# The words of w_out in the buffers of the probabilities and of the state product, with a new order of issue

## The chip, the core and the metric

One core of a Trainium2 chip runs the whole kernel in one launch. The metric is the device time of one execution in microseconds (us), as the median of several runs. TensorE is written PE (its weight loads PEld), VectorE DVE, ScalarE ACT, GpSimd POOL, and SyncE SP; SP issues every DMA here.

## What is computed

The kernel fuses a two-way attention between a sequence and a small state with a gated projection over the joined result.

```python
B, H, S, Ns, D = 8, 8, 512, 32, 64
scores  = scale * x @ state.T                 # 512 x 32 for each batch and head
xread   = softmax(scores) @ state
scores2 = scale * state @ x.T
sread   = softmax(scores2) @ x
y = concat([xread, sread], axis=2)            # to (batch, 576, 512)
gate_pre = sum(conv_w[k] * shifted(y, k) for k in range(5))
out = (sigmoid(gate_pre) * (y @ w_val)) @ w_out
```

The three weights w_val, conv_w and w_out arrive as 64-bit floats and are seen by the kernel as 64-bit words.

## The kernel before

A batch is one of eight. Its four x tiles are transposed on PE (`x_T`, tile xT), the scores of the 32 state rows are multiplied out (`long_scores` for batches 0 to 2, `scores` for the others, tile sc), and the softmax along the state rows follows on DVE, POOL and ACT: `scores_T` (tile sl), `max_n` (mx), `sub_n`, `exp_n` (ex), `sum_n` (sm, rc), `scale_n`, and `probs`, which transposes the probabilities back into sl (tile a0 for batch 0). The other softmax runs beside it (`max_s` with nb, `exp_s` with e, `exp_T`, `state_read` with srp). `state_val` (sgv, split into swh and swl) multiplies the state by w_val beforehand, so that `values` needs only the probabilities, split into a high part ah and a low part al. `read` (for batch 0 `read_conv` on z5) gives xr, the five taps of the gate run over it (`gate_first`, `gate_tap`, `gate_last`, `gate_add`, `gate`), `gated` makes the product g, which is split into gh and gl, and `project` multiplies by w_out, split into woh and wol. The last 32 rows of each batch, from sread, are done together at the end (`tail_values`, `tail_project`).

The weights come in as words. `load_words` brings 128 rows of a weight (512 KB) into an SBUF buffer, and five steps turn them into 32-bit floats: `words_scale` on ACT, `words_clamp` on DVE or POOL, and `words_low`, `words_join`, `words_sign` on DVE. A buffer of words is free when `words_sign` has read it. Tiles are made from pools of few buffers, and the table `alias` says which pool a short-lived tile takes its buffer from: "al" and "swl" (two buffers each, 4 KB a partition) hold the low parts of the probabilities and of the state product, "ah" and "swh" (two each, the same size) the high parts, and also a0 and sw0 of batch 0.

Each piece of work is a step with a number. `ORDER` lists the 938 step numbers in the order in which they are issued, with the engine for the steps that can run on several (a is ACT, v is DVE, g is POOL). Each engine runs its instructions in that order, and so does SP with its DMAs; an instruction that waits for a buffer or an operand holds up all that stands behind it on its engine. `warm_up` is a step of four small matmuls that nothing reads; 33 of them stand in the order.

```python
    with tc.manual_schedule(engines=None):
        for step in ORDER:
            engine = ENGINES.get(step[-1])
            fn, args = steps[int(step.rstrip("avg"))]
            fn(*([engine] if engine else []), *args)
```

Of the kernel before, what the change touches and what calls it, by code (L numbers as in the profile page):

```python
# [9 lines left out]
F32 = mybir.dt.float32  # L10
F32R = mybir.dt.float32r
I32 = mybir.dt.int32
# [16 lines left out]
LONG = (0, 1, 2)  # L29
ENGINES = dict(a="ACT", v="DVE", g="POOL")  # L30
ORDER = """
0 50 1 107 10 18 53 11a 65 41 42a 12 5 13g 14 43 23 7 35 44v 15 24a 45 36a 25 37 46 2 6 47 26v 29 915 916 917 918 919
920 921 922 923 924 925 926 927 928 929 930 931 932 933 934 48 114 38v 106 19 104 64a 105 27 39 30a 55a 115a 20a 89
935 112 28 4 113a 52a 31 16 108 185 54a 188 21 110 32v 109a 111a 33 936 120 51a 17 186 116 40 90a 34 189 91 195 49a
22a 122 62 56 191 123 92g 133 187 60v 193 286 118 77 119 287 121 59 285 190a 117 131 58a 288 57a 130 124 139 192a 196a
194a 93 134a 63a 125g 61a 141a 197 198 78a 71 66v 201 132a 184 291 199 94 293 79 103 8 126 292a 135 83 294a 127 68 385
295 296a 202 289 290a 200 388 128g 67a 101a 203 937 297 205 136 142g 129 80v 301 214 145 303 386 204 140a 143 302 299
387 146a 215a 84a 298 206g 486 213 151 207 216 208 304 86v 144 81 209v 85 69 70a 152a 168 137 150 217a 148 72a 82 222
153 147 154 487 155a 87 218 225a 73 284 156 74g 149a 219 210 138a 300 484 169 316 97a 75 88 227 76 211a 317a 228 160
170a 157 230 158a 226 223a 212g 485 95a 224 229a 159v 98g 164 231 165 314 250a 249 171g 235 256 220 583 315a 232 221a  # L40
389 391 390a 395 251 237 233g 166a 392a 252 396a 161 167g 393 394a 318 253 234 313 421 319 422a 397 238 96g 236a 264
257 402 384 423 254g 162a 99a 268 403 398 399 255 260 163g 401 239 400 269 258a 270a 305 100g 424a 102g 242 240v 322
306g 325a 243a 307 413 323a 414a 259g 425 181 326 241 172 244 494 245 182a 320 173a 246 308 309g 324 404 321a 415 261
492 483 493a 247g 495a 488 175 262a 310 263g 327 586 176v 311a 342 312v 343a 178 248 416a 328 405g 335 344 368 265
271g 585 345 346 266a 179a 406 347g 489a 330 356 348 350a 490 337 364 331 174 332 365 267g 329a 349 360 407 338 333g
275 272 682 491a 351 334 276a 339 352 357 520 183 408g 353 409 685 336a 273a 358a 340g 354g 523a 359g 410a 341 274 426
521v 524 281 582 366a 412 177 361 427 428a 584 411g 278 367g 429 522 362a 355 430 434 436 282a 683 496 431 369 363g
437 417 780 497 459 432g 279a 370a 448 435a 498 418 499 500 371g 449a 503 450 455 280 438 451 504g 587 433 456 439g
452 441 378 591 505 440 457a 506 283 507g 453g 501 460 372 588a 373a 684 443 502 508 375 379v 592a 442a 277 525 454
461g 376a 444 445 512 467 526 528 529 589 458g 446g 513a 468 514 593 533 463 509a 515a 447 530 784 462g 781 511 180  # L50
535 527a 381 547 548a 536 590a 419 549 594a 595 537 382a 420a 550 377 464 619 469g 531g 551 510g 465g 532 599 782 534a
692 540 600 470g 596 622a 686 687a 566 601 693a 597 552g 688 620a 598 602 603g 562 553 621 613 690 623 541a 689a 567
554 691a 542 516 466g 604 694 783 517 543 605 699 700 606g 374 544 545g 696 614a 695 607 568a 480 555 481a 697 546
569g 471 482 472a 473 624 608a 791 785 698 538v 610 380 563 639 641 642 643 556a 557g 474 786a 625 9 558 518 539 475a
789 632 701 640a 633v 627 609g 519a 564a 611 634 628 612a 790a 644g 645 681 477 626a 661 635 559 646 636 653 702g 703
478a 560a 648 787 629 565g 712 637g 479 792a 788a 561g 662 649 718 713a 793 881a 719a 615 704 663a 650 797 795 630g
638 616 794 879a 647a 885a 664g 886v 631 573 710 705g 654 798 570 721a 720 651g 800 617 574a 801g 706 711a 722 796
571a 799 809 655a 707a 709 657 618a 723 731 732a 808 714 715 658 733 725a 724 652 579 659a 476 580a 581 726 734 708g
727 716 656g 665 660g 735 810a 811 736g 883a 717a 764 802 745 812a 728 729g 747 666 576 748 667a 730 577a 813 738 803
740 749 817 752 383 818a 668g 741 804g 814 756 746v 672 753 750g 737 742 805 754a 739a 751 757 760 673a 822 819 758a  # L60
674 755g 743g 820v 765 821 806a 575 759v 675 678 766a 744 844 572 846 830 832 815 807g 761 847 669 679a 833 831a 767g
816v 848 851 834 762a 855 837 880g 884g 845a 835v 763g 839 859 849g 882g 836 676a 677 840 823 841 825 838v 863 887a
826 888v 777 771 827 899 900 842g 856 843 901 904 857a 824a 772a 774 850 680 858v 828v 773 860 670a 671 902 864 865a
861g 862g 903 894 866g 829 768 889 852 905 778a 853a 890 769a 779 906 895 854g 891 873 892 907a 870 908v 893 578 896
874a 897a 898v 867 871a 872 875 770 912 775v 913a 914 868v 869 909 876 776 910a 911 877a 3 878
""".split()


# [1 line left out]
def state_attention_gated_kernel(  # L70
# [41 lines left out]
        ah=(2, [P, NG, S], F32R), al=(2, [P, NG, S], F32R),  # L112
        swh=(2, [P, NG, C], F32R), swl=(2, [P, NG, C], F32R),
        acc=(3, [P, S], F32), last=(2, [P, S], F32), sig=(4, [P, S], F32),
        g=(2, [P, S], F32), gh=(7, [P, S], F32R), gl=(7, [P, S], F32R), o=(4, [P, C], F32),
        nb=(4, [P, NG], F32), sum2=(4, [P, NG], F32), r2=(2, [P, NG], F32),
        mx=(2, [P, NB, 1], F32), sm=(2, [P, NB, 1], F32), rc=(2, [P, NB, 1], F32),
        zc=(1, [P, TAPS, P], F32), cwf=(1, [TAPS * NPR, P], F32), cww=(1, [TAPS * NPR, 2 * P], I32),
    )

    alias = dict(
        wc=("g", F32), ws=("o", I32), sTl=("last", F32), z5=("zc", F32), vw0=("al", I32), vw1=("swl", I32), ow0=("al", I32), ow1=("swl", I32),
        sg=("acc", F32), a0=("ah", F32), sw0=("swh", F32),
        tacc=("last", F32), xth=("ah", F32R), xtl=("al", F32R), wvh=("x", F32R), wvl=("x", F32R), tsig=("sig", F32), tg=("g", F32), tgh=("gh", F32R), tgl=("gl", F32R), to=("o", F32),
        xTp=("ps", F32), e2p=("ps", F32), srp=("ps", F32), srT=("ps", F32), cwp=("ps", F32),
# [609 lines left out]
```

## Time and profile before

| | before |
|---|---|
| median of 3 runs | 241.32 us (241.07 to 242.23) |
| the profiled execution's own time | 241.91 us |
| its span, first to last instruction | 240.1 us |
| PE busy | 232.9 us, 97% |
| DVE busy | 188.1 us, 78% |
| ACT busy | 165.0 us, 69% |
| POOL busy | 131.5 us, 55% |
| DMA queue of SP | 22.57 MB, 30.9% of 16 engines' span |
| mean granted TensorE clock | 0.998 |

The profiled execution took 1.8 us more than its span and 0.6 us more than the median. PE's busy time counts the warm-up matmuls too: 132 of them, 18.8 us.

### The profile page before, as it was taken

The numbers are of one execution on the slowest core, as the hardware profiler recorded it, in microseconds if no ns is written. First come the engines' busy times: TensorE is split into PE (matmuls) and PEld (weight loads), VectorE is DVE, ScalarE is ACT, GpSimd is POOL, SyncE is SP. The second block draws the span as 40 slices with busy tenths as digits, with TensorE's granted clock in tenths as the row PEclk, the third lists the DMA queues.
The fourth block names the chain that finished last, engine by engine and source line by source line (L and its number), as shares of the span: only waits on it lengthen the run. The fifth ranks groups of instructions, "written<-read, shape, count | busy, mean of one in ns | idle before, by whom it ended". The sixth has DMA issues, their size and how long they took to land.

```text
span 240.1 us, 5167 instructions
## 1 busy us (share of the span) xinstructions
PE 232.9 (97%) x2015; PEld 175.7 (73%) x2015; DVE 188.1 (78%) x296; ACT 165.0 (69%) x348; POOL 131.5 (55%) x103
## 2 busy tenths in 40 slices
PE   6999999989999999999999999999999999999994
PEld 6997675546568686668686668867777688889883
DVE  2645799969999899699699987979589779965610
ACT  2327988789888794975799678897985746443311
POOL 3000436145786957956888567976868676052000
PEclk9999999999999999999999999999999999999999
DMA  5993998060002400637150012110020302022235
GB/s 182 312 357 118 296 242 183 19 141 15 3 0 60 114 3 1 187 109 212 44 135 0 3 44 101 46 44 1 3 87 3 131 0 90 1 87 87 75 100 177
DMA packets 34550, 22.90 MB, mean 95 GB/s; under 512 B 26058, under 2 KB 29150, under 8 KB 34526
## 3 DMA queue, kind: packets, MB, share of 16 engines
q1 hardware_dynamic: 34526, 22.57, 30.9%
q8 instruction: 16, 0.26, 0.5%
q14 instruction: 8, 0.07, 0.1%
HBM read 13.65 MB, written 8.91 MB: 94 GB/s over the span
## 4 chain that ended last, share of the span: by engine, by line
PE 86%; DVE 5%; ACT 4%; POOL 3%; issue 2%; ACTq 0%; POOLq 0%; DVEq 0%
PE val L484 17%; PE op L492 13%; PE op L494 12%; PE op L493 12%; PE warm L243 7%; PE xTp L309 5%; PE srp L365 3%; PE xr L421 3%; PE sgv L287 3%; PE tval L544 2%; PE e2p L355 2%; PE sc L315 2%; PE sc L337 2%; ACT xT L162 2%; POOL sl L175 1%
## 5 line engine op out<-in xcount | busy, mean ns | idle before, releaser
L461 DVE SCALAR_TENSOR_TENSOR acc<-xr,cw,acc 128x511 f32<-128x511 f32 (+2 forms) x84 | 59.7, 740 | 11.4 <-ACT xt L457 6.6
L492 PE MATMUL op<-woh,gh 128*128 128x512 f32 x128 | 51.6, 403 | 0.5 <-DVE swl L295 0.5
L494 PE MATMUL op<-woh,gl 128*128 128x512 f32 x128 | 50.3, 393 | 0.0
L493 PE MATMUL op<-wol,gh 128*128 128x512 f32 x128 | 50.1, 391 | 0.0
L175 POOL TENSOR_TENSOR gl<-g,gh 128x512 fp32r<-128x512 f32 x29 | 38.6, 1331 | 13.4 <-ACT gh L162 13.0
L175 POOL TENSOR_TENSOR acc<-acc,last 128x508 f32<-128x508 f32 x24 | 31.7, 1323 | 11.0 <-DVE acc L461 2.9
L492 PEld LDWEIGHTS op<-woh,gh 128*128 128x128 f32 x128 | 24.0, 188 | 8.7 <-DVE swl L295 1.3
L162 ACT COPY o<-op 128x512 f32<-128x512 f32 x28 | 16.5, 590 | 20.2 <-PE op L494 14.8
L494 PEld LDWEIGHTS op<-woh,gl 128*128 128x128 f32 x128 | 24.0, 188 | 5.4
L493 PEld LDWEIGHTS op<-wol,gh 128*128 128x128 f32 x128 | 24.1, 188 | 4.7
L487 DVE SCALAR_TENSOR_TENSOR g<-sig,val 128x512 f32<-128x512 f32 x32 | 21.6, 675 | 2.9 <-ACT sig L473 2.4
L484 PE MATMUL val<-ah,swh 128*128 128x512 f32 x56 | 23.4, 418 | 0.0
L162 ACT CAST gh<-g 128x512 fp32r<-128x512 f32 x28 | 17.5, 629 | 7.6 <-DVE g L487 7.6
L484 PE MATMUL val<-ah,swl 128*128 128x512 f32 x56 | 22.1, 394 | 0.0
L484 PE MATMUL val<-al,swh 128*128 128x512 f32 x56 | 22.0, 394 | 0.0
L456 ACT ACTIVATE acc<-xr,cw 128x512 f32<-128x512 f32 x28 | 19.4, 701 | 2.5 <-PE xr L421 2.3
L243 PE MATMUL warm<-ident 128*128 128x128 f32 x132 | 18.8, 303 | 1.8 <-POOL ident masks.py:199 1.8
L175 POOL TENSOR_TENSOR sl<-sl,mx 128x1024 f32<-128x1024 f32 x8 | 16.3, 2034 | 7.6 <-DVE mx L394 7.6
L162 ACT COPY xT<-xTp 128x512 f32<-128x512 f32 x32 | 18.1, 599 | 3.0 <-PE xTp L309 2.9
L473 ACT ACTIVATE sig<-acc 128x512 f32<-128x512 f32 x28 | 18.0, 644 | 2.7 <-POOL acc L175 1.9
L175 POOL TENSOR_TENSOR ex<-ex,rc 128x1024 f32<-128x1024 f32 x7 | 13.4, 1917 | 11.7 <-DVE rc L406 8.0
L243 PEld LDWEIGHTS warm<-ident 128*128 128x128 f32 x132 | 18.0, 218 | 2.1 <-POOL ident masks.py:199 1.8
(124 smaller groups left out, 457.2 us busy)
## 6 DMA issues: line engine op xcount, KB each, us to landing
x<-x SPq DMA_DIRECT2D x32, 256.0 KB
out<-o SPq DMA_DIRECT2D x32, 256.0 KB
vw<-w_val SPq DMA_DIRECT2D x4, 512.0 KB
ow<-w_out SPq DMA_DIRECT2D x4, 512.0 KB
sg<-state SPq DMA_DIRECT2D x8, 64.0 KB
z<-state SPq DMA_DIRECT2D x16, 32.0 KB
out<-to SPq DMA_DIRECT2D x8, 64.0 KB
cww<-conv_w SPq DMA_DIRECT2D x1, 20.0 KB
```

What stands on the lines that cost most here:

```text
L162: nc.scalar.copy(out, in_)
L175: (nc.vector if e == "DVE" else nc.gpsimd).tensor_tensor(out, a, b, op=how)
L243: nc.tensor.matmul(get("warm", i)[:, j * P:(j + 1) * P], ident, ident, start=True, stop=True)
L309: nc.tensor.transpose(get("xTp", b, pr)[:, j * P:(j + 1) * P], t, ident)
L456: nc.scalar.mul(get("acc", b, pr), pt, cw[:, HALO, pr:pr + 1])
L461: nc.vector.scalar_tensor_tensor(acc[:, d:], get("xr", b, pr)[:, :S - d], cw[:, HALO - d, pr:pr + 1], acc[:, d:], op0=ALU.mult, op1=ALU.add)
L473: nc.scalar.activation(get("sig", b, pr), get("acc", b, pr), AF.Tanh, scale=0.5)
L484: nc.tensor.matmul(get("val", b, k), w, a, start=(i == 0), stop=(i == len(parts) - 1))
L487: nc.vector.scalar_tensor_tensor(get("g", b, k), get("sig", b, k), 1.0, get("val", b, k), op0=ALU.add, op1=ALU.mult)
L492: nc.tensor.matmul(pt, gh, woh[:, k], start=(k == 0), stop=False)
L493: nc.tensor.matmul(pt, gh, wol[:, k], start=False, stop=False)
L494: nc.tensor.matmul(pt, gl, woh[:, k], start=False, stop=(k == NPR - 1))
```

## The change

The words of w_out are read into buffers of "ah" and "swh" in place of "al" and "swl". The words of w_val stay where they were, so the two weights no longer share buffers. `ORDER` is written anew from end to end: 930 steps, all but warm-ups the same ones, 25 warm-ups in place of 33, and about two dozen copies and splits that went to another engine.

```diff
@@ ORDER @@
-0 50 1 107 10 18 53 11a 65 41 42a 12 5 13g 14 43 23 7 35 44v 15 24a 45 36a 25 37 46 2 6 47 26v 29 915 916 917 918 919
+53 7 50 2 59 56 4 106 112 18 10 12 11a 23 29 13g 14 35 1 25 83 9 15 24a 5 31 8 26v 21 107 30a 19 22v 915 916 917 918
...
@@ alias @@
-        wc=("g", F32), ws=("o", I32), sTl=("last", F32), z5=("zc", F32), vw0=("al", I32), vw1=("swl", I32), ow0=("al", I32), ow1=("swl", I32),
+        wc=("g", F32), ws=("o", I32), sTl=("last", F32), z5=("zc", F32), vw0=("al", I32), vw1=("swl", I32), ow0=("ah", I32), ow1=("swh", I32),
```

What the new order does at the three places that matter below is seen in each engine's own list of instructions. First SP, from its sixth row on: x is a pair of x tiles or one tile (256 KB), vw and ow are the words of w_val and w_out (the number behind them is that of the weight's quarter), sg is the state of four batches, z the state of one. Before:

```order
L270 DMA sg_139<-state 32x8x64 x4
L199 DMA vw_1_145<-w_val 128x512
L186 DMA x_90<-x 128x2x256 x3
L199 DMA ow_3_235<-w_out 128x512
L186 DMA x_261<-x 128x2x256 x4
L186 DMA x_347<-x 128x2x256
L199 DMA ow_1_350<-w_out 128x512
L186 DMA x_347<-x 128x2x256 x3
L199 DMA ow_0_412<-w_out 128x512
```

Now:

```order
L199 DMA ow_2_124<-w_out 128x512
L186 DMA x_97<-x 128x2x256 x3
L270 DMA sg_188<-state 32x8x64 x4
L199 DMA vw_3_201<-w_val 128x512
L186 DMA x_219<-x 128x2x256
L199 DMA ow_1_222<-w_out 128x512
L186 DMA x_219<-x 128x2x256 x3
L186 DMA x_308<-x 128x2x256 x3
L199 DMA ow_3_396<-w_out 128x512
```

The first quarter of w_out moved ahead of batch 0's x, the state of the first group moved behind it, and the last quarter of w_val behind both.

Second PE, at the start: warm are warm-ups, xTp the transposes of x (the number behind the name is that of the pair of heads; x_90 and x_97 are batch 0), sgp the transposes of the first state group, cwbp and cwp small products for the convolution, sc the scores. Before, after 25 other warm-ups:

```order
L243 MATMUL warm_204<-ident 128x128 x2
L276 MATMUL sgp_207<-ident,sg_139 128x128 x4
L309 MATMUL xTp_3_212<-ident,x_90 128x128 x4
L259 MATMUL cwbp_219<-cwf,sel 128x128 x4
L243 MATMUL warm_237<-ident 128x128 x2
L309 MATMUL xTp_2_240<-ident,x_90 128x128 x4
L243 MATMUL warm_246<-ident 128x128 x2
L247 MATMUL cwp<-ident,cwf 128x20
L309 MATMUL xTp_0_256<-ident,x_90 128x128 x4
L259 MATMUL cwbp_265<-cwf,sel 128x128
L309 MATMUL xTp_1_267<-ident,x_90 128x128 x4
```

Now (where the dots stand are four and six more warm-ups of the same form):

```order
L309 MATMUL xTp_2_99<-ident,x_97 128x128 x4
L243 MATMUL warm_119<-ident 128x128 x2
...
L259 MATMUL cwbp_142<-cwf,sel 128x128
L259 MATMUL cwbp_147<-cwf,sel 128x128 x4
L243 MATMUL warm_153<-ident 128x128 x2
...
L309 MATMUL xTp_3_168<-ident,x_97 128x128 x4
L309 MATMUL xTp_0_174<-ident,x_97 128x128 x4
L309 MATMUL xTp_1_180<-ident,x_97 128x128 x4
L243 MATMUL warm_198<-ident 128x128 x2
...
L276 MATMUL sgp_246<-ident,sg_188 128x128 x4
```

One transpose of x stands after three warm-ups and the other three after thirteen, ahead of the state's, which stands after 21; two more warm-ups come between it and the first scores.

Third DVE, from the first scores of batch 0 on (sl and nb from sc, sum over states mx, words of w_out ws_o, words of w_val ws_v and wv). Before:

```order
L345 TENSOR_REDUCE nb_321<-sc_1_281 128x1
L172 TENSOR_SCALAR sTl_324<-sgp_207 64x4x32
L345 TENSOR_REDUCE nb_321<-sc_0_293 128x1
L388 STREAM_TRANSPOSE sl_355<-sc_1_281 128x512
L388 STREAM_TRANSPOSE sl_355<-sc_0_293 128x512
L372 TENSOR_SCALAR r_0_370<-sum_0_332 128x2
L373 RECIPROCAL r_0_370<-r_0_370 128x2
L394 TENSOR_REDUCE mx_373<-sl_355 128x32
```

Now:

```order
L388 STREAM_TRANSPOSE sl_300<-sc_0_269 128x512
L345 TENSOR_REDUCE nb_302<-sc_0_269 128x1
L388 STREAM_TRANSPOSE sl_300<-sc_1_278 128x512
L226 SCALAR_TENSOR_TENSOR ws_v_258<-wc_v_261,ws_v_258 128x512
L216 TENSOR_SCALAR ws_o_327<-ow_1_222 128x512
L394 TENSOR_REDUCE mx_329<-sl_300 128x32
L231 SCALAR_TENSOR_TENSOR wv<-vw_3_201,ws_v_258 128x512
L226 SCALAR_TENSOR_TENSOR ws_o_327<-wc_o_297,ws_o_327 128x512
L345 TENSOR_REDUCE nb_302<-sc_1_278 128x1
```

The transposes come first, one of the two maxima nb moved behind mx, and steps of the words stand in between.

## Rows read from the trace of the kernel before

**Rows 1.** Busy time by stretch; then PE's granted clock, DMA share, GB/s.
```profile
0.00:16.20 16.20, 14.39 (x106) 14.39 (x107) 7.21 (x16) 3.66 (x5) 2.17 (x13) 1.00 0.85 275
16.20:42.10 25.90, 25.30 (x356) 17.79 (x356) 19.80 (x35) 21.66 (x50) 8.93 (x7) 1.00 0.80 221
42.10:62.20 20.10, 18.97 (x257) 11.20 (x251) 17.86 (x28) 16.95 (x39) 8.87 (x7) 1.00 0.23 51
62.20:236.30 174.10, 173.63 (x1319) 131.90 (x1302) 143.22 (x218) 122.18 (x253) 111.49 (x77) 1.00 0.20 65
236.30:240.10 3.80, 0.58 (x5) 0.39 (x3) 0.00 (x0) 0.59 (x1) 0.00 (x0) 0.88 0.31 104
```

**Rows 2.** Timeline of PE: start, us, line, operation, tiles.
```profile
1.81 14.39 PE L243 MATMUL warm<-ident 128*128 128x128 f32 x104 [1.81 <-POOL ident masks.py:199]
...
21.81 2.23 PE L337 MATMUL sc<-xT,sTl 128*32 128x256 f32 x32
...
37.74 4.87 PE L436 MATMUL xr<-a,z 32*64 32x512 f32 x80
...
48.77 1.98 PE L484 MATMUL val<-a,sw 128*128 128x512 f32 x4 [0.63 <-DVE g L487]
```

**Rows 3.** The chain that ended last: start, us, what. Lengths of dense pieces.
```profile
103.53 1.02 PE sc L315 x16
104.55 1.03 PE srp L365 x64
...
108.56 0.44 PE xTp L309 x4
...
117.71 1.04 PE xr L421 x16
...
129.34 1.40 PE val L484 x6
...
147.42 0.45 PE warm L243 x4
```

**Rows 4.** Waits of SP's own queue: waited for, us in total, times, longest.
```profile
SPq L199 <- DVE wv L231: 7.5, 2, 6.8
```

**Rows 5.** The same columns as rows 1, for the first 14 us.
```profile
0.00:6.00 6.00, 4.19 (x19) 4.20 (x20) 1.30 (x3) 1.60 (x2) 2.17 (x13) 1.00 0.57 182
6.00:8.00 2.00, 2.00 (x16) 2.00 (x15) 1.40 (x4) 0.68 (x1) 0.00 (x0) 1.00 0.95 322
8.00:10.00 2.00, 2.00 (x20) 2.00 (x19) 0.67 (x2) 0.69 (x1) 0.00 (x0) 1.00 0.97 256
10.00:12.00 2.00, 2.00 (x20) 2.00 (x19) 1.59 (x4) 0.69 (x1) 0.00 (x0) 1.00 1.05 356
12.00:14.00 2.00, 2.00 (x20) 2.00 (x19) 2.00 (x5) 0.00 (x0) 0.00 (x0) 1.00 1.06 371
```

**Rows 6.** Timeline of DVE: start, us, what; in brackets the wait before it.
```profile
10.41 0.43 DVE L216 TENSOR_SCALAR ws_v<-vw 128x512 int32<-128x512 int32 x1 [1.16 <-DMA vw<-w_val]
...
26.95 1.20 DVE L394 TENSOR_REDUCE mx<-sl 128x32 f32<-128x1024 f32 x1
28.06 0.69 DVE L226 SCALAR_TENSOR_TENSOR ws_o<-wc_o,ws_o 128x512 int32<-128x512 int32 x1
...
32.29 1.22 DVE L404 TENSOR_REDUCE sm<-ex 128x32 f32<-128x1024 f32 x1
...
33.76 0.35 DVE L406 RECIPROCAL rc<-sm 128x32 f32<-128x32 f32 x1
34.03 0.65 DVE L388 STREAM_TRANSPOSE sl<-sc 128x512 f32<-128x512 f32 x1
...
36.30 1.22 DVE L412 STREAM_TRANSPOSE a<-ex 128x1024 f32<-128x1024 f32 x1
```

**Rows 7.** Timeline of POOL, the softmax of batch 0.
```profile
28.23 2.29 POOL L175 TENSOR_TENSOR sl<-sl,mx 128x1024 f32<-128x1024 f32 x1 [2.78 <-DVE mx L394]
...
34.26 1.91 POOL L175 TENSOR_TENSOR ex<-ex,rc 128x1024 f32<-128x1024 f32 x1 [3.74 <-ACT xT L162]
```

More of the change, by code (lines that the diff above doesn't have):

```diff
@@ L31 @@
 ORDER = """
-0 50 1 107 10 18 53 11a 65 41 42a 12 5 13g 14 43 23 7 35 44v 15 24a 45 36a 25 37 46 2 6 47 26v 29 915 916 917 918 919
[L33 to L65, printed above, removed]
+53 7 50 2 59 56 4 106 112 18 10 12 11a 23 29 13g 14 35 1 25 83 9 15 24a 5 31 8 26v 21 107 30a 19 22v 915 916 917 918
@@ new lines @@
+919 114 104 108 105 110 32v 27 33 47 84a 86v 36a 0 41 37 111a 38v 85 115a 87 28 109a 20a 39 88 188 40 77 34 920 921
+922 923 924 925 926 48 113a 52a 3 51a 43 54a 42a 6 185 55v 187 116 120 58v 186 61a 195 66a 78a 62 117 118 57a 44g 121
+65 287 927 928 189 193 45 79 124 191 119 80g 190a 196a 60a 194a 131 192a 201 46 81 285 122 67a 197 203 288 16 64a 99a
+125g 132a 202 289 123 89 133 286 293 63a 71 103 126 130 82 290a 127 49a 929 291 204 388 295 198 292a 128g 199 296a 216
+205 294a 217a 142g 139 17 129 301 134a 303 72a 184 297 206g 298 140a 68 200 299 90a 135 73 92v 141a 207 143 214 74v
@@ new lines @@
+150 91 215a 136 304 387 208 153 93 75 164 145 144 209v 97a 94 101a 210 300 100g 160 165 76 148 147 213 102g 154 146a
+69 149a 227 155a 386 70a 166a 235 161 314 316 249 168 162a 302 237 229a 95a 315a 305 167g 151 137 163g 385 98g 306g
+169 218 138a 211a 228 251 156 238 252 219 484 152v 389 239 253 317a 393 236a 395 157 390a 230 231 240g 394a 391 392a
+222 232 396a 225a 223v 212g 241 250a 322 397 226 318 485 242 224 260 170a 244 96g 284 325a 245 158a 171g 326 402 268
+159g 403 254g 261 307 246 255 256 262a 401 308 399 309g 243a 486 323a 324 269 172 310 233g 400 173a 270a 220 221a 181
@@ new lines @@
+182a 313 247g 398 487 384 271g 404 327 413 234 263g 311a 586 342 319 344 328 175 414v 345 336a 248 494 495a 343a 264
+415 257 330 405g 176a 488 492 346 584 490 335 258a 265 331 178 406 491v 416a 417 347g 337 489a 332 348 312g 493a 329a
+338 407 496 349 339 179a 483 351 259g 421 500 364 174 365 498 422a 501 266a 267g 352 408g 340g 360 585 502 353 499
+366a 424a 281 180 333g 497 350a 423 275 341 282a 409 354g 334 276a 425 368 426 361 320 412 511 503 321v 367g 355 362a
+427 434 583 272 429 418 369 436 441 587 683 589 410a 278 504g 430 443 505 370a 431 588a 444 593 363g 590a 183 445 428a
@@ new lines @@
+591 279a 411g 442a 682 506 356 512 177 273a 514 685 592a 446g 357 437 594a 595 371v 515a 432g 455 358a 277 463 438 600
+447 599 435a 597 283 448 450 433 513a 596 601 459 359g 507g 378 449a 464 439g 598 456 274 684 611 690 602 457a 603g
+451 465a 379a 458g 688 280 440 452 686 689a 691a 582 508 780 604 687a 419 420a 372 520 460 781 783 373a 525 453g 454
+523a 612v 605 466g 782 526 606g 547 540 524 549 381 692 784 509a 521a 550 382a 528 693a 551 374 467 461a 529 548a 375
+607 542 510g 694 552g 527a 608a 530 522 468 462g 376a 516 543 613 699 696 534a 566 517 469a 554 562 544 553 700 533
@@ new lines @@
+531g 883g 377 470g 614a 541a 789 567 532 791 695 535 697 787 790a 698 609g 792a 555 788a 545g 619 681 536 383 624 537
+568a 569g 701 620a 622v 633a 480 546 621 538g 785 639 702g 632 563 539 625 634 477 635 481v 564a 478a 565g 712 641 623
+636 637v 556g 557g 703 627 482 628 471 474 629 879a 640a 713a 472a 638 475a 709 704 518 558 559 519v 786a 646 705g 648
+615 476 793 626a 657 560a 561g 880g 794 661 630g 479 631 706 642 798 658 643 649 570 659a 795 571a 610 710 799 647a
+797 579 616 650 660g 711a 580v 617 800 644g 723 653 645 581 662 738 739a 665 885g 796 651g 573 652 740 732v 886g 741
@@ new lines @@
+724 663a 666 731 801g 802 574a 742 733 811 726 734 618a 667a 664g 743g 576 707a 668g 654 714 727 735 728 655a 812a
+656v 725a 718 803 817 744 473 745 747 575 675 380 748 708g 721v 577a 749 722 736g 578 669 719a 820a 729g 804g 884g 720
+760 572 715 756 746v 678 821 737 670a 676a 761 818a 809 805 822 730 808 750v 762a 679a 810a 806a 813 844 830 716 757
+752 845a 677 819 763g 758g 759g 814 838v 846 751 847 807g 753 848 849g 881a 717a 837 839 764 672 765 754a 766a 840
+755g 850 859 680 831v 767g 841 863 882g 832 864 815 823 816v 833 825 855 826 673v 842g 824v 768 834 865a 887a 843 866g
@@ L66 @@
+827 888g 860 861a 828v 862g 777 774 829 775a 894 851 890 835v 900 771 836 892 904 769a 889 895 852 905 776 772a 773
+856 899 891 853a 854v 770 857a 858g 876 893 896 671 870 902 778a 873 901 897a 898v 903 874a 906 907v 877a 674 908v 779
+909 910v 875 878 871v 912 911 913a 872 914 867 868a 869
 """.split()
```

## The prediction

> **What bounds the kernel now.** I read first the busy time by stretch. From 62.2 us on PE is busy for 173.63 of 174.10 us, and DVE (143.22), ACT (122.18) and POOL (111.49) have room there [rows 1]; so that part is as long as PE's work, and a change can shorten it only by taking work from PE. The timeline of PE shows what the busy figure hides at the start: until 16.2 us PE runs 104 warm-ups and nothing else, the first scores start at 21.81 us and the convolved read of batch 0 at 37.74 [rows 2]. Between 16.2 and 62.2 PE is called busy for 44.27 of 46.0 us [rows 1], but much of it is small matmuls that stretch until an operand comes. I therefore measure PE by the work itself, with the lengths that pieces have where they stand back to back in the chain of waits: four transposes 0.44, the scores of a late batch 1.02, `state_read` 1.03, `read` 1.04, one `values` 1.40 [rows 3]; a `values` of batch 0 takes about 1.95 [rows 2]. Every step of PE is in both orders except warm-ups, so the end moves by as much as the start of the dense part does.
>
> **The words' buffers.** Before, w_out's quarters had to wait in SP for the buffers of w_val's words: 6.8 us at the longest wait, for the DVE step that reads the last words of w_val [rows 4]. Behind that wait stood x of batch 2, two more quarters and z. It goes: no DMA of SP up to batch 4's x waits for another engine now, only for earlier DMAs. What it gives by itself I put at 0, since the first scores need batch 0's x and the first state group, both ahead of that wait. In its place stands a shared use with a0 and sw0: a0 takes the buffer of w_out's first quarter, whose words DVE reads before the first scores. I put this at 0 too; the cover is that a0 is written at about 33 us, and it would cost one for one only if that quarter were read later than that.
>
> **When batch 0's data are there.** The bytes that had moved are 1.09 MB at 6 us, 1.74 at 8, 2.25 at 10, 2.96 at 12, 3.70 at 14 [rows 5]. Before, the last of batch 0's x was byte 3.43 MB of the queue, the state group byte 2.12. Now a quarter of w_out (0.52 MB) goes ahead of three pairs of x, but a quarter of w_val and the state went behind them: the last x is byte 3.17 MB, reached at 12.6 us, and the state byte 3.43 MB, at 13.3. A transfer ends later than its bytes suggest when several are in flight: the third quarter of w_val was byte 1.86 MB, reached at 8.5, and DVE saw it at 10.41 [rows 6]. So x is there between 12.6 and 14.5 and I take 13.7, the state between 13.3 and 15.2.
>
> **PE's start.** Warm-ups pass at about 0.2 us each up to 6 us and at 0.1 from 8 us on (19 in the first 6 us, then 16, 20 and 20 in 2 us) [rows 5]. PE now reaches the second x transpose after 62 matmuls, at about 10.7 us; its pair of x is byte 2.64 MB, reached at 11.1 us and so there by 13.0 at the latest: a wait of 0.4 to 2.3 us. The last transposes end at 14.1; eight warm-up steps (32 matmuls) take 3.5, the state's transposes 0.44: 18.1. Then ACT and DVE write sTl (0.3 each, three on ACT, 0.9) while two warm-ups pass: the first scores start at 19.1, with a bound of 18.0 to 20.0 from x, against 21.81. The state has 2.5 us of cover in the eight warm-ups.
>
> **The softmax of batch 0.** Before, from the first scores to the write of a0: 21.81 to 36.30, 14.5 us [rows 2, 6]. Now in DVE's order: the first scores end at 20.1; sl, nb, sl at 0.65, a join of words 0.61, a shift of words 0.35, mx 1.2, and a hand-over of 0.3 make mx end at 24.4 (before 28.15 [rows 6]). POOL's subtraction takes 2.29 [rows 7]: 26.8. The exponential waits instead for the other softmax, since ACT runs one `exp_s` before it and that one's maximum now stands behind two steps of words: 24.4 + 1.2 + 0.65 = 26.3, `exp_s` 0.7, one copy 0.3, so it runs from 27.3 to 28.4. The sums take from 32.29 to 34.11 before [rows 6], 1.8 with the reciprocal: 30.3. POOL's scaling takes 1.91 and came 0.15 later [rows 7]: 32.4. On DVE a `scores_T`, an nb and the mx of batch 1 (0.65, 0.65, 1.2) end at 32.8 and are now the last to end; a0 follows until 34.0, and `read_conv` starts at 34.2 against 37.74. **Term one: -3.5 us.** PE has done the same work by then in both orders (20.7 us of it), so nothing of this is borrowed.
>
> **From there to the dense part.** Before, the work of 42.1 to 62.2 us adds up to 18.4 of 20.1 us by the lengths above; 1.13 of the 1.7 lost are idle [rows 1], among them 0.63 for the first g [rows 2]. Now `read_conv` ends at 38.6; up to `values` of batch 1 there are 18.0 us of work. I allow 0.8 for the first `values` of batch 0, which waits for a PSUM buffer behind two ACT copies (0.4 to 0.5 each). sl of batch 1 has to be ready for `read` at 44.8: DVE, from 34.0 with a0, has some 9 us of work before it (among it 3 us of w_out's words), 43. POOL's al is ready at 55.5 for 57.4. **Term two: 0.8 - 1.7 = -0.9 us.** PE then starts `values` of batch 1 at 57.4.
>
> **Later.** One warm-up in the middle of the dense part goes, 0.45 us [rows 3]. **Term three: -0.45 us.** The copies that went from ACT to DVE or POOL I put at 0: all three have 30 us or more to spare after 62.2 us [rows 1]. The end stays: last copy, last store, 3.8 us after PE [rows 1].
>
> **The sum.** 3.5 + 0.9 + 0.45 = 4.85. The profiled execution goes from 241.91 to 237.1 and its span from 240.1 to 235.3; the median of the runs, 0.6 lower than that execution, from 241.32 to 236.5.
>
> **Rivals.** *The clock falls.* PE now idles up to 2.3 us near 11 us, where it never idled. Warm-ups at 0.2 us instead of 0.1 would then cost 3.4 on the 34 or so matmuls behind it and 0.8 on the next ones: scores at 23.3, term one down to about +0.7, and 240.7 in all. For it: the pace did begin at half [rows 5], 1.2 against 2.4 GHz. Against: before, 0.6 us idle at 48 us changed nothing [rows 2], though that wait was shorter. The Trainium skill, "TensorE: Matmul & The Clock Gate", Part 1, says that the low clock is what an idle engine falls back to and that activity lifts it; by that rule the wait is the danger and the warm-ups of the old start were worth their place. No row here shows a wait long enough to decide it.
>
> *The state lands late.* It stands behind x and is made of 256-byte pieces; if it came at 18 instead of 15 the cover is used up, and each further microsecond costs one. At 20, 238.9. The Trainium skill, "DMA: Bandwidth & Descriptors", Specifications, asks for 512 bytes or more for full rate; the rate did fall to 256 GB/s at 8 to 10 us, when the state was on its way [rows 5], which agrees.
>
> *Slower: DVE becomes the bound.* In the new order 55.0 us of DVE's work stand before the second `probs` after a0 (sl of batch 2), for `read` of batch 2 on PE at about 67. My chain has it at 65.4, with 10.4 us of idle DVE before. Before, DVE idled 17.3 of the first 62.2 us [rows 1], 28%. At 28%, 55.0 us take 76.2: PE would wait 9 us, the gain turn to a loss of 4.5, and the time be 245.8. It decides from an idle time of 17 us on. Against it: DVE's steps of words now fill the idle time of the start.
>
> *Half given back.* The dense part lost some 2.7 us to small waits before (174.1 for 171.4 of work); a tighter order may lose 2.5 more in places that I did not follow: 239.0. Or it loses none: 234.3.
>
> *The buffers do nothing.* Only the order counts, and w_out's words come early for nobody; the time is the same as in the forecast, 236.5.
>
> **How the numbers follow.** Forecast (the buffers' idle case with it) 0.58, half given back 0.15, none lost 0.08, clock 0.08, late state 0.04, DVE 0.07. The range goes from just under 234.3 to the clock's 240.7. What a measurement can tell from no change is about 0.5%, 1.2 us: below 240.1 is faster, above 242.5 slower. Faster: 0.58 + 0.15 + 0.08 + 0.04 = 0.85, less 0.02 for slips; same: 0.08 and 0.02; slower 0.07.
>
> **What would show it.** Right: first scores of batch 0 at 18 to 20 us, `read_conv` near 34, `values` of batch 1 near 57, PE without a wait over 1 us after it, no wait of SP for DVE among the first thirty DMAs. Wrong: warm-ups between 14 and 18 us at 0.2 us, `sgp` later than 18.5 behind a DMA, or `read` of batch 2 waiting for sl.

## The result, and the profile after

The changed kernel takes 238.41 us (median of 3 runs, 238.18 to 239.36) against 241.32: a ratio of 0.9884, 95% interval 0.9851 to 0.9917. The forecast was 236.5 with a range of 234.0 to 240.7: faster as foretold, by 2.9 us where 4.85 were forecast. A later set of six runs gave 238.16 against 241.28 (0.9881, 0.9854 to 0.9909). The profiled execution has a span of 237.6 us, 2.5 less than before.

The timeline of PE in the changed kernel answers to [rows 2]:

```profile
12.20 0.63 PE L309 MATMUL xTp<-ident,x 128*128 128x128 f32 x4 [1.02 <-DMA x<-x]
...
14.51 3.74 PE L243 MATMUL warm<-ident 128*128 128x128 f32 x32
18.08 0.60 PE L276 MATMUL sgp<-ident,sg 128*128 128x128 f32 x4
...
19.51 1.93 PE L337 MATMUL sc<-xT,sTl 128*32 128x256 f32 x32
...
29.81 0.75 PE L355 MATMUL e2p<-ident,e 128*128 128x128 f32 x4 [1.23 <-ACT e L348]
...
37.00 4.53 PE L436 MATMUL xr<-a,z 32*64 32x512 f32 x80
...
61.01 0.50 PE L484 MATMUL val<-ah,swh 128*128 128x512 f32 x1
```

The start went as foretold. PE waited 1.02 us for x (forecast 0.4 to 2.3), 32 warm-ups passed in 3.6 us, and the first scores stand at 19.51 (forecast 19.1, before 21.81). Then the forecast is lost: `read_conv` starts at 37.00 and not at 34.2. From the first scores to it the new order takes 17.5 us, the old one took 15.9.

DVE's timeline answers to [rows 6]:

```profile
22.63 1.33 DVE L226 SCALAR_TENSOR_TENSOR ws_v<-wc_v,ws_v 128x512 int32<-128x512 int32 x1
...
24.22 1.21 DVE L394 TENSOR_REDUCE mx<-sl 128x32 f32<-128x1024 f32 x1
...
25.95 2.40 DVE L226 SCALAR_TENSOR_TENSOR ws_o<-wc_o,ws_o 128x512 int32<-128x512 int32 x1
28.27 1.27 DVE L345 TENSOR_REDUCE nb<-sc 128x1 f32<-128x512 f32 x2
...
35.01 1.23 DVE L412 STREAM_TRANSPOSE a<-ex 128x1024 f32<-128x1024 f32 x1
```

POOL's timeline answers to [rows 7]:

```profile
22.81 0.61 POOL L221 TENSOR_SCALAR wc_o<-wc_o 128x512 f32<-128x512 f32 x1
25.51 2.29 POOL L175 TENSOR_TENSOR sl<-sl,mx 128x1024 f32<-128x1024 f32 x1 [2.09 <-DVE mx L394]
```

ACT's timeline shows what waits for it:

```profile
28.98 0.69 ACT L348 ACTIVATE e<-sc,nb 128x512 f32<-128x512 f32 x1 [1.43 <-DVE nb L345]
```

A join of words takes 0.68 to 0.69 us while POOL rests (lockfree2 below). Here one takes 1.33 beside POOL's clamp and one 2.40 beside POOL's subtraction, and ends 0.5 us after it (25.51 + 2.29 = 27.80). No row reports a wait of these steps: both engines are shown as busy. The second nb stands behind the long join, so the second `exp_s` on ACT waits 1.43 us for it, and PE 1.23 us for that.

Busy time by stretch answers to [rows 1]:

```profile
0.00:19.51 19.51, 16.26 (x119) 15.32 (x119) 9.75 (x22) 7.49 (x15) 2.46 (x13) 1.00 0.90 289
19.51:37.00 17.49, 15.60 (x234) 10.71 (x233) 16.76 (x26) 14.78 (x35) 8.16 (x8) 1.00 0.67 199
37.00:61.00 24.00, 23.10 (x344) 11.99 (x337) 23.05 (x37) 20.00 (x47) 14.43 (x10) 1.00 0.34 76
61.00:233.80 172.80, 172.78 (x1303) 132.34 (x1295) 141.14 (x222) 116.37 (x242) 111.09 (x76) 1.00 0.21 67
```

From 19.51 to 37.00 DVE is called busy for 16.76 of 17.49 us; part of that is standing still. The dense part is full: 172.78 of 172.80. Among SP's waits none of [rows 4] is left. By places, the span's 2.5 us are 2.3 gained up to the first scores, 1.6 lost from there to `read_conv`, 0.6 gained from it to the first values of batch 0 (5.3 us for 5.9), and 1.2 gained behind them.

### The profile page after: what moved, and what is told of

It is laid out like the page before. It is cut to its first block, busy times and chain, and to the rows that moved or that the text cites. A ratio compares the mean times of both kernels' runs of the same rounds, so it can differ in the third digit from the quotient of the medians.

```text
span 237.6 us, 5105 instructions
## 1 busy us (share of the span) xinstructions
PE 227.9 (96%) x1983; PEld 170.4 (72%) x1983; DVE 190.7 (80%) x305; ACT 159.2 (67%) x336; POOL 136.1 (57%) x106
## 4 chain that ended last, share of the span: by engine, by line
PE 80%; DVE 10%; DMA 3%; SPq 2%; ACT 2%; issue 1%; POOL 0%; ACTq 0%; POOLq 0%; DVEq 0%
PE val L484 18%; PE op L492 13%; PE op L494 12%; PE op L493 12%; PE xTp L309 4%; DMA x<-x 3%; PE srp L365 3%; PE sgv L287 3%; PE xr L421 3%; PE tval L544 2%; PE sc L315 2%; PE e2p L355 2%; PE warm L243 2%; DVE ws_o L226 1%; SPq L186 1%
## 5 line engine op out<-in xcount | busy, mean ns | idle before, releaser
L175 POOL TENSOR_TENSOR gl<-g,gh 128x512 fp32r<-128x512 f32 x29 | 38.1, 1319 | 25.8 <-ACT gh L162 25.6
L175 POOL TENSOR_TENSOR acc<-acc,last 128x508 f32<-128x508 f32 x24 | 31.2, 1307 | 7.4 <-DVE acc L461 4.3
L162 ACT COPY o<-op 128x512 f32<-128x512 f32 x28 | 16.4, 593 | 26.5 <-PE op L494 24.4
L162 ACT CAST gh<-g 128x512 fp32r<-128x512 f32 x30 | 18.7, 629 | 6.9 <-DVE g L487 6.9
L309 PE MATMUL xTp<-ident,x 128*128 128x128 f32 x128 | 17.6, 279 | 1.6 <-DMA x<-x 1.6
L162 ACT COPY xT<-xTp 128x512 f32<-128x512 f32 x31 | 17.2, 602 | 2.8 <-PE xTp L309 2.8
L175 POOL TENSOR_TENSOR sl<-sl,mx 128x1024 f32<-128x1024 f32 x8 | 15.7, 1965 | 5.6 <-DVE mx L394 3.9
L175 POOL TENSOR_TENSOR al<-sl,ah 128x1024 fp32r<-128x1024 f32 x7 | 16.9, 2412 | 2.5 <-ACT ah L162 2.5
```

The source lines that it names most:

```text
L162: nc.scalar.copy(out, in_)
L175: (nc.vector if e == "DVE" else nc.gpsimd).tensor_tensor(out, a, b, op=how)
L309: nc.tensor.transpose(get("xTp", b, pr)[:, j * P:(j + 1) * P], t, ident)
```

## Experiments

Each was compared with the kernel before on the same chip; the chips differ from row to row, so rows are compared by the ratio. Places in the program are given as us from the span's start in the profiled execution. All but before, own_before, start_new and start_old have the changed kernel's order on PE except for warm-ups, so there a shift of one matmul is a shift of PE's work; own_before has the old order, and start_new and start_old have a half of each.

| kernel | us | ratio to before (95%) | first scores | read_conv | first values of batch 0 | span |
|---|---|---|---|---|---|---|
| before | 241.32 | | 21.8 | 37.7 | 43.6 | 240.1 |
| changed | 238.41 | 0.9884 (0.9851–0.9917) | 19.5 | 37.0 | 42.3 | 237.6 |
| after_again | 238.16 | 0.9881 (0.9854–0.9909) | 17.8 | 35.3 | 40.6 | 235.8 |
| no8 | 236.59 | 0.9814 (0.9789–0.9838) | 16.3 | 33.8 | 39.1 | 234.4 |
| lockfree | 237.55 | 0.9848 (0.9828–0.9868) | 17.9 | 33.8 | 40.7 | 235.7 |
| both | 236.68 | 0.9806 (0.9780–0.9832) | 16.8 | 32.7 | 39.6 | 234.6 |
| lockfree2 | 237.03 | 0.9820 (0.9791–0.9850) | 18.2 | 34.6 | 39.9 | 235.2 |
| both3 | 236.49 | 0.9785 (0.9764–0.9807) | 16.8 | 32.9 | 38.2 | 234.2 |
| both2 | 236.26 | 0.9786 (0.9767–0.9805) | 17.2 | 33.6 | 38.9 | 234.2 |
| own_before | 241.59 | 1.0003 (0.9988–1.0019) | 21.2 | 37.2 | 43.0 | 239.5 |
| no_warm | 239.74 | 0.9919 (0.9889–0.9949) | 18.4 | 37.3 | 42.5 | 237.8 |
| start_new | 242.87 | 1.0050 (1.0033–1.0066) | 18.3 | 35.8 | 41.1 | 240.8 |
| start_old | 249.70 | 1.0338 (1.0305–1.0371) | 22.2 | 38.2 | 44.0 | 249.5 |
| pool_hold | 238.59 (one run) | | 18.6 | 36.2 | 41.5 | 236.8 |

**after_again**, no edit. 

> The changed kernel once more, as the reference of the runs beside it. 238.4 us, 2.9 below the kernel before, if the first timing was no accident; PE's first scores at 19.5 us, read_conv at 37.0, the first values of batch 1 at 61.0.

 The time came out, the places did not: the first scores started 1.7 us earlier, since PE did not wait for x in this execution, and everything behind moved by the same 1.7. The two profiled executions took 239.36 and 237.66 us, and all of their difference lies ahead of the first scores. All six runs spread by 2 us (237.66 to 239.63), and stretches are compared below from the first scores on: 17.5 us to `read_conv` and 22.8 to the first values, in both executions alike.

**no8**, the eight warm-up steps ahead of the state's transposes.

```diff
-... 40 77 34 920 921 922 923 924 925 926 48 113a ...   (and step 0)
+... 40 77 34 48 113a ...
```

> Leaves out the eight warm-up steps (32 matmuls, 3.6 us) between the last x transposes of batch 0 and the state's transposes; nothing that is computed changes. Theory: they are all that holds the first scores back, since the state was there at 15 us. The state's transposes start at 15.0 instead of 18.1, ACT is busy with x copies until 17.2 and DVE with words until 17.4, so the first scores start at 17.9 to 18.1 instead of 19.5, and all that follows comes 1.5 us earlier: 236.9. Rival one: PE's clock falls without the warm-ups; then the granted clock reads 0.5 in a stretch from 16 us on and the gain is lost: 238 to 239.5. Rival two: behind the scores the chain waits for batch 1's x, which lands at 20 to 21.5 us, and the gain shrinks to 0.5 or less: 238.

```profile
13.43 0.63 PE L275 MATMUL sgp<-ident,sg 128*128 128x128 f32 x4 [0.33 <-DMA sg<-state]
...
16.34 1.94 PE L336 MATMUL sc<-xT,sTl 128*32 128x256 f32 x32 [1.39 <-issue]
```

```profile
14.00:16.00 2.00, 0.95 (x9) 0.76 (x7) 2.00 (x5) 1.98 (x6) 0.00 (x0) 1.00 1.00 326
16.00:18.00 2.00, 1.66 (x32) 1.13 (x32) 1.32 (x4) 1.37 (x4) 0.00 (x0) 1.00 1.07 380
```

These are PE's timeline of no8 (the lines of code are one up) and two of its stretches, in the columns of [rows 1]. 236.59 is 1.6 below the changed kernel, the first theory; the clock stayed at 1.00 through PE's wait of 1.39 us, and the stretch to the first values stayed 22.8. The first scores stand 1.4 us ahead of those of after_again, where x came early too. That is less than the 3.6 us of the warm-ups, since PE now waits 0.33 us for the state and 1.39 before the scores, while ACT still copies x; it begins sTl at 15.69. My prediction had priced the warm-ups (3.5 us) and not asked what they were worth.

**lockfree**, DVE's words away from POOL.

```diff
-62 117 118 57a 44g 121 65 ... 79 124 191 119 80g 190a ... 201 46 81 285 ... 132a 202 289 ... 126 130 82 290a 127
+62 44v 117 118 57a 121 80v 65 ... 79 124 191 119 190a ... 201 285 ... 132a 202 46 289 ... 126 130 290a 81 127
...
-17 129 301
+17 129 82 301
...
-100g 160 ... 102g 154
+160 ... 102g 100g 154
```

> Same work in the changed kernel, but DVE's two-operand steps of words no longer stand beside POOL: the clamps of w_val's and w_out's words go from POOL to DVE, two joins and a sign behind the first scores_T of batch 1, one sign behind the write of a0, one low half of w_out on POOL back by one place. Theory (a DVE step with two SBUF operands stands still while POOL's instruction runs): joins at 0.7 instead of 1.33 and 2.40 us, mx of batch 0 ends at 24.4 instead of 25.4, the second nb starts near 24.5 instead of 28.3, read_conv at 35.2 to 35.8 instead of 37.0; time 236.6 to 237.2. Rival: the long steps are a wait for an operand or a late instruction, and PE's own queue bounds the stretch; then they stay long where they stand now, and the time is 238.4 within 0.4. The Trainium skill, 'SBUF — State Buffer', 'SBUF: two separate sides', says that the port which DVE and GpSimd share is an exclusive lock, held for a whole instruction; this kernel is to show it.

 `read_conv` started 15.95 us behind the first scores instead of 17.50, as the lock theory says, joins took 0.68, and POOL's subtraction 1.91:

```profile
23.47 1.91 POOL L175 TENSOR_TENSOR sl<-sl,mx 128x1024 f32<-128x1024 f32 x1 [2.83 <-DVE mx L394]
```

The edit also moves two steps of words out of the second nb's way, so it doesn't price the lock alone. An estimate from the rows of the changed kernel: at 0.68 the long join would have ended 1.7 us earlier and the second nb with it, which covers ACT's wait of 1.43. So the lock alone can account for most of the 1.55 us.

But the first values came 22.77 behind the first scores, unchanged to 0.01. The rows of PE and the wait of ACT show why:

```profile
33.84 6.12 PE L436 MATMUL xr<-a,z 32*64 32x512 f32 x80
```

```profile
ACT sw L170 <- DVE ws_o L231: 1.8, 1, 1.8
```

My edit had put the sign step of w_out's second quarter behind a0. sw0 now takes the buffer of that quarter's words, so ACT waited 1.8 us for the step, the PSUM buffer of sgv that one tile of xr takes came free late, and `read_conv` ran for 6.12 us instead of 4.53. That is the sharing that the change brings in. The prediction looked at a0 and found it harmless; for sw0 it holds only as long as the sign step stands early.

**both** is that order without the eight warm-ups. 

> The two edits together: without the eight warm-up steps, and with the words' steps moved away from POOL. If both theories hold and don't share a gain: first scores near 18.0, read_conv near 33.8, 235.2. If batch 1's x (lands at 20 to 21.5 us) or ACT's copies bound the stretch then, the sum shrinks to that of one: 236.5.

 236.68: the start's gain alone, since the other half had been lost to sw0's wait.

**lockfree2** mends it (the diff is against lockfree).

```diff
-132a 202 46 289 ... 126 130 290a 81 127 49a
+132a 202 46 81 82 289 ... 126 290a 127 130 49a
...
-17 129 82 301
+17 129 301
```

> As lockfree, but the sign step of w_out's second quarter stands ahead of batch 0's sums again instead of behind the write of a0. In lockfree that step held the buffer that sw0 takes, ACT waited 1.80 us for it, and read_conv, which needs the PSUM buffer that sw0's copy frees, ran for 6.12 us instead of 4.53. Theory: read_conv starts 15.9 to 16.1 us behind the first scores as in lockfree and runs for 4.5, the first values of batch 0 come 21.2 to 21.4 us behind the first scores instead of 22.8, and the time is 236.2 to 236.6. Rival: the gain is lost again at the read of batch 1 or its values, since POOL and DVE are no earlier there: 237.5, as lockfree.

 DVE's timeline, and PE's:

```profile
21.50 0.69 DVE L226 SCALAR_TENSOR_TENSOR ws_v<-wc_v,ws_v 128x512 int32<-128x512 int32 x1
...
27.54 0.68 DVE L226 SCALAR_TENSOR_TENSOR ws_o<-wc_o,ws_o 128x512 int32<-128x512 int32 x1
...
36.48 0.75 DVE L221 TENSOR_SCALAR wc_o<-wc_o 128x512 f32<-128x512 f32 x2
```

```profile
34.60 4.54 PE L436 MATMUL xr<-a,z 32*64 32x512 f32 x80 [0.37 <-DVE a L412]
...
39.87 1.98 PE L484 MATMUL val<-a,sw 128*128 128x512 f32 x4
```

The same joins take 0.69 and 0.68 where 1.33 and 2.40 stood, two clamps together 0.75 where 1.84 stood, and the first values come 21.7 us behind the first scores (22.8 before the edit). This gain is kept to the end: from the first values to the end of the span it is 195.3 us, as in the changed kernel. The time, 237.03, is 0.4 above the range that I expected: `read_conv` stands 16.4 us behind the first scores instead of 16.0, since the sign step now delays the sums. Against the changed kernel the edit gives 1.1 us by the places (22.8 to 21.7), and 1.5 by the ratios, 0.9881 and 0.9820, whose intervals don't overlap.

**pool_hold** turns the theory round: POOL's work is put beside DVE's steps, with no data, buffer or order of theirs touched.

```diff
+    def hold(e):
+        t = xt[:, :, :, HALO:]
+        one = ones[:, 0:1].unsqueeze(2).unsqueeze(3).broadcast_to(list(t.shape))
+        for i in range(4):
+            combine(e, t, one, one, ALU.mult)
...
-... 29 13g 14 ...
+... 29 13g 965g 14 ...
```

> The changed kernel with four instructions on POOL that nobody waits for, right behind the clamp of the convolution's words: each writes 128 x 1024 numbers from a column of ones into the convolution's tail buffer, which is overwritten later. They are to run from about 4.5 to 12 us, beside DVE's steps of w_val's words; no data, no buffer and no order of these steps is touched. Theory (a DVE step on SBUF stands still while a POOL instruction runs, and the other way round): steps of words that take 0.42 and 0.68 us alone take 1 to 2.3 us there, or POOL's instructions take more than 1.91 us each; steps that start after 12.5 us are unchanged. Rival (the long steps in the changed kernel were waits for operands): all steps keep 0.42 and 0.68. The time may rise by 0 to 3 us, since DVE's words end later than 17.4 us.

 POOL's timeline (the four together, then the second and the third by themselves) and DVE's:

```profile
4.12 8.72 POOL L175 TENSOR_TENSOR xt<-ones 128x1024 f32<-128x1024 f32 x4
...
6.08 2.16 POOL L175 TENSOR_TENSOR xt<-ones 128x1024 f32<-128x1024 f32 x1
...
8.32 2.49 POOL L175 TENSOR_TENSOR xt<-ones 128x1024 f32<-128x1024 f32 x1
```

```profile
4.18 1.97 DVE L226 SCALAR_TENSOR_TENSOR ws_conv<-wc_conv,ws_conv 20x128 int32<-20x128 int32 x1 [0.50 <-POOL wc_conv L221]
6.08 0.41 DVE L216 TENSOR_SCALAR ws_v<-vw 128x512 int32<-128x512 int32 x1
6.41 1.97 DVE L231 SCALAR_TENSOR_TENSOR cwf<-cww,ws_conv 20x128 int32<-20x128 int32 x1
...
9.23 1.86 DVE L221 TENSOR_SCALAR wc_v<-wc_v 128x512 f32<-128x512 f32 x1
11.01 2.98 DVE L226 SCALAR_TENSOR_TENSOR ws_v<-wc_v,ws_v 128x512 int32<-128x512 int32 x2
```

Steps on 20 x 128 numbers, 0.28 us in the changed kernel, take 1.97: as long as POOL's instruction beside them (1.88 to 2.49 each). The pair of joins takes 2.98 (1.28 alone). The short step that starts at 6.08, together with the second POOL instruction, is not delayed, and that POOL instruction takes 2.16 instead. From 13.3 us on, behind POOL's last, all steps have their usual length until POOL works again at 20.8. The edit left their operands as they were, so a wait for an operand is ruled out. The time, 238.59 in one run, is near that of the changed kernel: DVE's words ended at 19.6 us instead of 17.4, and little waited for them (`read_conv` came 17.7 us behind the first scores instead of 17.5).

**own_before** asks what the buffers alone do, in the old order.

```diff
+        own=(1, [P, NG, S], F32),
...
-            get(f"{tag}{k % 2}", k) ...
+            get("own" if (tag, k) == ("ow", 1) else f"{tag}{k % 2}", k) ...
```

> The kernel before, in its own order, but the quarter of w_out that SP held longest (the second) has a buffer of its own; the other three stand where they stood. So SP's wait of 6.8 us is gone and nothing else is changed. The prediction's step (the buffers alone give nothing, since all that the first scores need is ahead of that wait): 241.3 within 0.5, first scores at 21.8 us, read_conv at 37.7. Rival (what stood in SP behind that wait, batch 2's x and the other quarters, held ACT, DVE or PE up later): 240.3 or less.

```profile
SPq L203 <- DVE wv L235: 0.7, 1, 0.7
```

Of SP's wait of 7.5 us [rows 4] 0.7 is left, and the time is 1.0003 of before: nothing, in the old order. The new order with the old buffers was not tried, so what the buffers are worth to the new order is not shown.

**start_new and start_old** were to divide the gain at 65 us (each is one order up to its 334th step, the other behind it). 

> The changed kernel up to its 334th step (PE is then at the read of batch 2, near 65 us), and from there on the order of the kernel before, without its warm-up step in the dense part. The prediction put 4.4 of its 4.85 us into the start: by that 238.4 and no more to gain later, as the changed kernel itself. The traces say that the start gave 1.2 to 2.9 us (first values of batch 0 at 40.5 to 42.3 against 43.5) and the rest of the order 1.3: by that 239.0 to 240.0, and the stretch from the first values of batch 0 to PE's end is 196 us instead of 195.3.

 

> The other half: the kernel before with its buffers up to its 334th step, and then the order of the changed kernel, without the warm-up step in the dense part. By the prediction 240.9 (only the 0.45 us of the warm-up step is saved later). By the traces 240.0: 1.3 us are saved behind 62 us, the warm-up step among them.

 They failed at that: the orders don't fit at the joint. start_new's PE is busy for 7.95 of the 10 us from 70 on, start_old's idles for 5.96. Two things can be read all the same. Behind the joint start_new runs the old order without its warm-up step: from its 90th matmul of `values` to the end 110.2 us (240.8 less 130.6) against 110.7 before (240.1 less 129.4), so that step cost 0.5 at most. And start_old shows the clock, which the next run takes up:

```profile
80.00:82.00 2.00, 0.58 (x8) 0.37 (x16) 1.93 (x2) 0.65 (x1) 2.00 (x3) 0.50 0.00 0
...
84.00:86.00 2.00, 2.00 (x6) 1.62 (x5) 1.62 (x3) 2.00 (x6) 1.58 (x1) 0.50 0.00 0
86.00:88.00 2.00, 2.00 (x11) 1.55 (x10) 0.53 (x1) 0.06 (x1) 0.00 (x0) 0.87 0.00 0
```

After PE had stood still from 75.5 to 81.4 us the granted clock was 0.50 (1.2 GHz), and matmuls of 512 columns passed at 0.43 us instead of 0.23 until 86.5.

**no_warm** leaves out eighteen of the 25 warm-ups (three of the first ten, not two). 

> The changed kernel without the warm-up steps 10 to 24 and two of the first ten: all those of the start between the convolution's matmuls and the scores, and the three behind the first scores. Nothing that is computed changes. It is to price the rival of the prediction in which PE's clock falls: PE then waits 1 to 4 us at a time before x, the state and the first scores. In start_old a wait of 5.96 us was followed by a granted clock of 0.50, and matmuls of 512 columns passed at 0.43 us instead of 0.23 until 86.5 us. If the clock falls here too, the start's 14 us of PE work up to read_conv go at half speed in part: 2 to 8 us more than without the eight warm-up steps alone, 238.5 to 244. If it does not fall: 236.2 to 236.6, as without the eight.

```profile
12.31 2.89 PE L308 MATMUL xTp<-ident,x 128*128 128x128 f32 x12 [2.76 <-DMA x<-x]
...
18.45 3.23 PE L336 MATMUL sc<-xT,sTl 128*32 128x256 f32 x32 [2.39 <-issue]
```

```profile
10.00:12.00 2.00, 0.00 (x0) 0.00 (x0) 1.10 (x3) 0.81 (x2) 0.00 (x0) 0.72 1.09 323
12.00:14.00 2.00, 1.69 (x8) 1.48 (x9) 1.97 (x6) 0.40 (x1) 0.00 (x0) 0.50 1.00 313
...
22.00:24.00 2.00, 1.91 (x17) 1.67 (x16) 1.59 (x2) 1.98 (x7) 1.58 (x4) 1.00 1.06 410
```

PE waited 2.76 us for x, the clock fell within this wait (0.72 from 10 to 12 us) and stayed at 0.50 until about 21 us; twelve transposes took 2.89 us and the first scores 3.23 instead of 1.93. Against no8 the ratio is 0.0105 worse, 2.5 us. So the eight warm-ups behind x don't earn their place, and some of the others do. That it is those ahead of x is my reading, since the clock fell there; the groups were not taken out one by one.

**both3 and both2** are the eight warm-ups and lockfree2's order together; both3 also has mx of batch 1 behind a0 (the diff is from both2 to both3).

```diff
-216 205 294a 217a 142g 139 17 129 301
+216 294a 217a 142g 139 17 129 205 301
```

> A version that is to beat both kernels: lockfree2's order, without the eight warm-up steps ahead of the state's transposes, and with mx of batch 1 behind the write of a0 instead of ahead of it (in lockfree2 a0 ended the wait of read_conv by 0.37 us). Sum of the parts by theory: eight warm-ups 1.5, the words' steps away from POOL 1.1, mx 0.3, together 2.9 below the changed kernel: 235.3 us; read_conv 15.9 to 16.1 us behind the first scores, the first values of batch 0 another 5.3 behind it. Rival: batch 1's x or the words of w_out land too late for the earlier scores, and the sum stays at 236.5.

 

> both3 without its last move: mx of batch 1 stands ahead of the write of a0 again. In both3 it came 1.4 us later, the second softmax with it, and PE waited 0.88 us for the second g behind that softmax's write on DVE. Theory: read_conv 16.4 us behind the first scores (both3 16.1), the first values of batch 0 at 21.7 (21.4), but no wait for g, and PE's end 217.0 behind the first scores (both3 217.45): 236.0 if the first scores start at 16.8. Rival: PE waits for g or for the read of batch 1 all the same: 236.5, as both3.

 both3 gained 0.3 us up to the first values and lost it again at a new wait, which both2 does not have:

```profile
43.41 0.66 PE L275 MATMUL sgp<-ident,sg 128*128 128x128 f32 x4 [0.88 <-DVE g L486]
```

Behind mx of batch 1 its whole softmax is late, and g stands behind that on DVE. Both spans are 234.2; their times, 236.49 and 236.26, can't be told apart. Either beats the changed kernel by 1%, and is as fast as the forecast for the changed one. The sum that I expected for both3 (235.3) was not reached: x and the state held PE for 1.3 us at its start (0.42, 0.46 and 0.38), and the new wait took back what mx gave.

## Why the prediction was right in direction and too large in size

The forecast in its own terms, for the profiled execution: the first scores 0.4 us later than forecast, the softmax up to `read_conv` 2.4 longer (17.5 for 15.1), from there to the first values of batch 1 0.8 longer (24.0 for 23.2), and the rest 1.3 shorter (176.6 for 177.9). Together 2.3: 237.6 for 235.3.

- **The buffers, 0.** Right in the old order: own_before. In the new order it stays open. The sharing with sw0, which I counted as harmless, is so in the changed order and costs 1.6 us in `read_conv` when one step is moved (lockfree).
- **PE's start.** Right within its bounds (18.0 to 20.0; 19.5, and 17.8 where x came early). That the state had cover behind the warm-ups is right too, and the cover was pure loss: 1.6 us by the times of no8, 1.4 by its places.
- **Term one, -3.5 us: mis-sized, the main error.** It measured -0.7. I took DVE's and POOL's steps at their lengths alone (0.61 for a join, 2.29 for POOL's subtraction) and laid them side by side. The joins can't lie beside POOL's steps: they became 1.33 and 2.40, the second nb and `exp_s` came late, and `read_conv` with them. lockfree takes 1.55 of the missing 2.4 back by moves of steps of words.
  The remaining 0.85 is PE's own: two waits for ACT's copies (0.41 and 0.18), and work that fills more than my whole 15.1. In lockfree PE is busy for 15.28 of the 15.94 us from the first scores to `read_conv`:

```profile
17.90:33.84 15.94, 15.28 (x234) 10.68 (x234) 14.19 (x26) 13.15 (x31) 6.32 (x6) 1.00 0.75 223
```

  It was 15.33 before and is 15.35 in lockfree2. The sum has the first scores over after 1.0 us, the length of the late batches [rows 3]. `long_scores`, which stands three times in this stretch, takes 1.93 each time, and [rows 2] had 2.23 for it. So the old order, at 15.9, was nearly full on PE already, and the 0.8 us that my sum takes off the softmax were not there to be had while PE had this work to do. Three warm-ups (some 1.5 us) are part of it; no run takes out these alone.
  The sign of the lock was in my own rows: POOL's subtraction took 2.29 us beside a join [rows 7], and it takes 1.91 without one (lockfree). I read the 2.29 as its length. The Trainium skill, "SBUF — State Buffer", section "SBUF: two separate sides", says that DVE and GpSimd share one pair of ports as an exclusive lock: a DVE step in a mode that uses both ports, or one with two SBUF inputs against a GpSimd instruction that reads SBUF, can't run together with that instruction, and whichever starts first keeps the pair to its end. pool_hold agrees in both directions (1.97 for 0.28 on DVE, 2.49 for 1.88 on POOL). So do the steps that kept their lengths: mx beside POOL's scaling 1.20, nb from PSUM 0.65.
- **Term two, -0.9.** Too large: by the 0.8 above it measured -0.1. PE waited 0.35 us for g and 0.49 for ACT's copy of e2T. Two clamps of w_out took 1.84 us beside POOL's split, but the lock is not shown to have cost anything here: in lockfree2 they take 0.75, and from `read_conv` to the first values of batch 1 it is 24.0 us all the same (34.60 to 58.60). The wait for e2T is still 0.48 there, and `read` of batch 1 runs for 1.60 instead of 1.17. What would give the 0.8 back stays open.
- **Term three, -0.45.** Right for the warm-up step (0.5 at most, by start_new). But the rest of the order gained some 0.7 more behind the first values of batch 0 (196.5 us to the end before, 195.3 after). About 0.5 of it stands in the one wait that the profile before reports for PE between 62 and 236 us, ahead of 97.75; the changed kernel has none there:

```profile
PE op L492 <- DVE swl L295: 0.5, 1, 0.5
```

  Which of the moves removed it, and where the rest went, is not shown: 55 steps changed engine (not about two dozen), 25 of them away from ACT and 13 to it.
- **The rivals.** The clock did not fall at a wait of 1.02 us, nor at 1.39 and 1.47 (no8, both2); it did at 2.76 and 5.96 (no_warm, start_old). My price for it, some 4 us, compares with 2.5 in no_warm. The mechanism was real, and no wait of this kernel set it off. The half pace of the first warm-ups, which I took as a sign of it, stands in [rows 5] at a granted clock of 1.00, so those rows don't tie it to the clock. "Half given back" came near in number (239.0), but named the dense part as the place, and that part gained.

## What to carry to other kernels

When DVE and POOL work side by side on SBUF, don't add their lengths as if each were alone: look for a DVE step that takes twice its usual time with no wait reported, and put such steps into POOL's pauses; POOL's own steps can stand beside DVE's reductions, which kept their lengths here. Then add up the work of the engine that comes next, at the lengths of the very pieces that stand there. Ask of every warm-up what would run in its place: without most of them the clock fell at a wait for x, and the eight behind x only delayed. When words or other passing data borrow a buffer, the step that frees it becomes part of the borrower's critical path: follow it before moving it.

## What was not expected of the hardware

A DVE step of 20 x 128 numbers can take 1.97 us, seven times its length, for no other reason than a POOL instruction that started 0.06 us earlier (pool_hold). And the landing of the same DMAs in the same order moves by 1 to 2 us between executions: PE had the last x of batch 0 at 14.05 us in the changed kernel, at 13.38 in both2, 12.95 in both3 and 12.47 in no8. Two profiled executions of the changed kernel differ by 1.7 us for this reason (first scores at 19.5 and 17.8).
